# Key features of the late head pairs in strided order: key sums through one DRAM write and read, key-value sums placed by one transfer

## Chip, cores and metric

One core of a Trainium2 chip runs the kernel. The metric is the device time of one execution in microseconds (us); of several executions the median is taken. Before the change it is 1027.04 us, the median of 3 runs (1024.86 to 1032.23).

## What is computed

Linear attention with exponential features over 8 batches x 8 heads of 576 tokens with 64 values each, and then a two-layer feed-forward part over the 4608 tokens. All of it in float32:

```python
def phi(x):
    proj = np.einsum('bhsd,df->bhsf', x, w_phi)                 # 64 -> 128 features
    proj = proj - np.max(np.abs(proj), axis=-1, keepdims=True)
    return np.concatenate([np.exp(proj), np.exp(-proj)], axis=-1)
q_p, k_p = phi(q), phi(k)
kv  = np.einsum('bhsf,bhsd->bhfd', k_p, v)                      # key-value sums
z   = np.sum(k_p, axis=2)                                       # key sums
num = np.einsum('bhsf,bhfd->bhsd', q_p, kv)
den = np.einsum('bhsf,bhf->bhs', q_p, z)[..., None] + 1e-06
x   = (num / den), tokens x 512
out = relu(x @ w_in)**2 @ w_out                                 # 512 -> 2048 -> 512
```

The order in which the 128 features are summed doesn't matter to kv, num, z and den, as long as keys and queries meet feature by feature.

## The kernel before

**Work and stages.** Heads are handled in 32 pairs (`p`), four to a batch. The feed-forward part takes tokens in 18 chunks of 256 and its 2048 inner columns in 8 pieces (`f`); each (chunk, piece) is a first product on TensorE (L1028, 24 matmuls), squares on ScalarE (ACT, L1037 to L1047) with a difference on VectorE (DVE, L321), and a second product (L1066, 12 matmuls). For the last six chunks the first product is a Strassen form over two chunks at once (L1206). The weights arrive in 32-bit words of 8-byte elements and are joined and split in the first 120 us (L468 to L543).

**Early and late pairs.** Pairs 0 to 5 are "early": everything including the key sums is done with matmuls. Pairs 6 to 31 are "late". TensorE serves late pairs in "visits" (`visit`), each of which does three things for three neighbouring pairs: keys of pair p+1 (`k_main` L599 and `k_tail` L605, through `lhsT` = keys and `rhs` = the projection weights `wst` / `wbf`), queries and key-value sums of pair p (L869, L877, L657, L662), and numerators of pair p-1 (L889). A visit's keys then go through DVE (maximum L615, subtraction L618) and ACT (two exponentials, L621 and L623).

**Key sums of a late pair** (`late`). After DVE has folded the exponentials over tokens into `es` (L638 to L648), it transposes them in 32x32 blocks (L954) and sums rows (L955) into `z4`, 128 partitions x 16. What is left is a sum over four groups of 32 partitions, and a layout with one feature per partition. Four transfers (L961, `gather`) bring the four partition groups beside each other in `za` (32 partitions), DVE adds them (L968, `zr`), and four more transfers (L965, `column`) spread the result to `zc`, 128 partitions x 4. `zc` then scales the query features: ACT L990 and DVE L992, for each head; GpSimd (POOL) sums them over partitions (L996), and the denominators go through DRAM and back (L998, L805, L806, L809, L816) to DVE (L823), which divides; L842 and L845 write the result as two float16 halves into `ring`, from which the first product reads.

**Key-value sums of a late pair** (`turn`). DVE transposes them in 32x32 blocks (L938), one transfer writes them to DRAM (`td`, L939), and four transfers (L944, `place`) read them into `kz`, the stationary operand of the numerators, each for one block of 32 features.

**What sets the order.** Every instruction is an `Op` of a `Plan`: its engine, an expected duration, what it waits for, and for transfers an issue time and a landing time. `order` simulates the engines with these numbers and always takes the ready operation of lowest rank; ranks of the attention part come from the string `RANKS` (two characters each). The outcome is a fixed program order on each engine. Engines then run their own lists strictly in order: a transfer that waits in the SP queue holds all that are listed behind it, and so does a waiting instruction on ACT or DVE. All DMAs are issued from SP. Where the plan leaves TensorE idle in the first 125 us, `zeros` (L1314) fills in matmuls on zeros.

Of the kernel before, what the change touches and what calls it, by code (L numbers as in the profile page):

```python
# [307 lines left out]
def tile_kernel(ctx, tc, qp, kp, vp, w_phi, w_in, w_out, out):  # L308
    nc = tc.nc
    V, A, G, PE, SP = nc.vector, nc.scalar, nc.gpsimd, nc.tensor, nc.sync  # L310
    P = Plan()
# [16 lines left out]
    def tiles(pool, tag, shape, dtype, bufs, first=0):  # L328
        return Tiles(P, pool, tag, shape, dtype, bufs, first)
# [5 lines left out]
    wbf, wst = wraw[:, 0:2 * F], wraw[:, 2 * F:]  # L335
# [13 lines left out]
    es_ = tiles(ap, "es", [128, 1024], F32, 1, EARLY)  # L349
# [3 lines left out]
    kz_ = tiles(ap, "kz", [128, 384], F32, 2)  # L353
# [233 lines left out]
    exps, exp_t, sums, kz_of, qexp, dens_of, k_load, q_load, num_in = {}, {}, {}, {}, {}, {}, {}, {}, {}  # L587
# [5 lines left out]

    def k_main(p, to):
        for t in range(4):
            for h in range(2):
                PE.matmul(out=to(h)[:, 128 * t:128 * t + 128],  # L599
                          lhsT=k_[p][64 * h:64 * h + 64, 128 * t:128 * t + 128],  # L600
                          rhs=wst[64 * h:64 * h + 64, :], start=True, stop=True)

    def k_tail(p, to):
        for h in range(2):
            PE.matmul(out=to[64 * h:64 * h + 64, :], lhsT=k_[p][:, 512:576],  # L605
                      rhs=wbf[:, 128 * h:128 * h + 128], start=True, stop=True)
# [329 lines left out]
    def turn(p, v, key, src, rank):  # L936

        o = P.add("DVE", dve_us(256), lambda: V.transpose(kvs_[p][:, 0:256], src()), [v], [key, ("kvs", p)], rank)  # L938
        o = P.add("SP", 0.4, lambda: SP.dma_start(  # L939
            td_[p].rearrange("s p x -> p s x"), kvs_[p][:, 0:256].rearrange("p (s x) -> p s x", s=2)), [o], [("kvs", p), ("td", p)], rank, land=1.9, xfer=0.1)  # L940

        def place():
            for b in range(4):
                SP.dma_start(kz_[p][32 * b:32 * b + 32, 0:256].rearrange("p (a x) -> p a x", x=32),  # L944
                             td_[p].rearrange("s (a i) (b x) -> b i (s a) x", a=4, b=4)[b])

        kz_of[p] = P.add("SP", 1.9, place, [o], [("td", p), ("kz", p)], rank, land=1.5, xfer=0.4)

    def late(p):

        rank = PER_PAIR * p + RA
        R = lambda x: rank + x

        o = P.add("DVE", dve_us(512), lambda: V.transpose(es_[p][:, 512:1024], es_[p][:, 0:512]), sums[p], [("es", p)], R(RZ))  # L954
        o = P.add("DVE", dve_us(512), lambda: V.tensor_reduce(  # L955
            out=z4_[p], in_=es_[p][:, 512:1024].rearrange("p (b x) -> p b x", x=32), op=ALU.add, axis=AX.X),
            [o], [("es", p), ("z4", p)], R(RZ))

        def gather():
            for a in range(4):  # L960
                SP.dma_start(za_[p][:, a, :], z4_[p][32 * a:32 * a + 32, :])  # L961

        def column():
            for b in range(4):
                SP.dma_start(zc_[p][32 * b:32 * b + 32, :], zr_[p][:, 4 * b:4 * b + 4])  # L965

        o = P.add("SP", 1.6, gather, [o], [("z4", p), ("za", p)], R(RZ), land=1.9, xfer=0.1)
        o = P.add("DVE", 0.23, lambda: V.tensor_reduce(  # L968
            out=zr_[p].rearrange("p (b j) -> p j b", b=4), in_=za_[p].rearrange("p a (j b) -> p j b a", b=4), op=ALU.add, axis=AX.X),
            [o], [("za", p), ("zr", p)], R(RZ))  # L970
        zc = P.add("SP", 1.6, column, [o], [("zr", p), ("zc", p)], R(RZ), land=1.9, xfer=0.1)
        pt = pt_of[p]
        qexp[p], dens = [], []
        for h in range(2):
            n = 2 * p + h
            qe = lambda s, n=n: qe_[n][:, S * s:S * s + S]
            o = P.add("POOL", par_us(S), lambda n=n, h=h: G.partition_all_reduce(  # L977
                mx_[n], pt_[p][:, h, :], channels=128, reduce_op=bass_isa.ReduceOp.absmax),
                [pt[h], pt[2], pool_next], [("pt", p), ("mx", n)], R(RQ + 0.2), lock=1.0)
            o = P.add("DVE", dve_us(S), lambda n=n, h=h, qe=qe: sub(V, qe(0), pt_[p][:, h, :], mx_[n]),  # L980
                      [o], [("pt", p), ("mx", n), ("qe", n)], R(RQ + 0.3), lock=4.0)
            o = P.add("ACT", act_us(S), lambda qe=qe: A.activation(out=qe(1), in_=qe(0), func=AF.Exp, scale=-1.0),
                      [o], [("qe", n)], R(RQ + 0.4))
            o = P.add("ACT", act_us(S), lambda qe=qe: A.activation(out=qe(0), in_=qe(0), func=AF.Exp),
                      [o], [("qe", n)], R(RQ + 0.4))
# [3 lines left out]
            y = lambda h=h: (rb_, ds_)[h][p]  # L989
            o = P.add("ACT", act_us(S, 1), lambda h=h, qe=qe, y=y: A.activation(  # L990
                out=y(), in_=qe(0), func=AF.Copy, scale=zc_[p][:, 2 * h:2 * h + 1]), [zc, o], use, R(RQ + 0.8))
# [345 lines left out]

DIGITS = "".join(chr(c) for c in range(33, 127) if chr(c) not in "\"\\'")[:90]
RANKS = (
    ">i<,KT011@Odd$J72uZ6DE=3QkK9NWh|HZLvUfYqOs67=jqd@-<Z6JGO7ra68E7{aYQaV,cwW:l/IKE7C_jsE4@C/&m&g<F4LXb_"  # L1340
    "aQmB@tC.=*sX]hv:a6z:O^odzfit64YdXe/`Sl`#?]d]a4AW2eWS.cOUnGKdm{FzSS@Xp}/={$i+]Aa]?uI0q*K-B^v}P3IA82=v"
    "]@<OotUk{:PXG[4C.0R/N[/`fLEqW/F]vzg]=[H44Za`FqSl.-dDDu5d9N1mG5>_m37CDLmNN;sbrPEr@G/,?RZI2(BTddfmzups"
    "off5Jt?rLN?_qg:i8#67C0/=;vVd[SKVOv^Ow0.}7hLnN=N?X*@N`}5mNlIj=HCaBf<aMEdf.H2C8wCc.8R(5Sr]?Z.o_k7.5|xG"
    "BF8P47Z<Ov1(F4`A[9TdJ4fXcC642ql*hBA(BytbUUZ5e?Q>CqOOWniO3=E<NVJm=F:m0o7Th5pHwI<=u,I#^k=jK=B1R].-]@T|"
    "D:lh/v{kK4cX6Z49Sj2-NiKL.-j]0/U{fUG6.nv7Xz1/`7[*^c<(l8.Ps_pXK@.-A`0?P#.bC]C>^i3,AQ?`MzUIa!.-lrA*i-Ss"
    "B#?`GdE>L!0SX]SAQ:L.9GJ&;;hkI5RO;<O2L>|t{nL,9>I57`OFC(Gw`;|[.o89.kKixhhUw=H8s;G37WveEWf+]nLl;-QdI5XE"
    ":7@@JYH-1mxyU!V{UT.3kUKIFCa}q%<tD/ME0]3W0bEX@.|t0dmZmLILKmKR|t<Jp7<>F@9xscF)9,rJ34^fYeDLBnFt.IW>f7J&"
    "2hP}jYl.o`j<kKhsW%L5dc7MtF.->*VcEdCFDD_>1D<*os_^QVI)KZA3HTK(9tBrA.th;M=)VWqeV&Z6r*ZJ<XgkB9^mx[c+:M:1"
    "2^T/_|5E7$8fF^l4RTt>Ex3dH;D_RBig9HlOL;m|DfInD}CHC(DfW]UD7x1|=*yrvE<4Lmx[ZQLi/V.-0v.-N-jO1:.IsLMQp15u"
    "2bq{C#^iLN2YGYt6AMH}bQ@j;wkf1&BlU|d]7#TLPz<y?AiKY`V<L7RW]ye=V*].@9A[Iw@v?B_m/iM$tsA%YHbbI59]JO<)V]Y5"  # L1350
    "LwCWplB-fza>nyi<Lw<o3zZ4Ki8MV}@[HPW|>*dRpE.-|Q=5w:T@xNRDxnQs<6lftH<[fQ5{YDGU=Wo%1e{,Ku5+v@.-<<1RD<:>"
    "TvpT/t|t9(XFX@uYsaaW|tP)AZsqP.4@Ck[_BSa79VjkF>d}LiO%KL8H[&h]R0lZ?8Nbl(EN.zu-1d[[ExquOa97X(56EkG&7Md#"
    "?>.Y:PBmH6[1zeen:5b[H*cZ5u@yp?_r6>@)FW=o0VFa?^V:`1sRurr2gR``4P:$w;[Lpm?>3T.-JJ6.YW[G_Kzym%btEf.-=cIp"
    ";D:b:[v!6lJ?8Zk_3{Ef^DeWV4Mb.-f8=)i)hgJmXmwQO/H)f;|kRiV?GKFyDQC)O+i@zHr}QQ3hA&p?;ZCD8!Hn3y42hAc&D:{|"
    ".DF[<4s965sCKW=lqY]`2Z7@U6Vb@-^z<(GhbruKU@3b:_Wwq3j43=Po1tIwNyhzRW[,Axh#wRecP|9hgv]z88L)yTJWsT3#bF]9"
    "@3Ky.}/]QHT=0Zt7H/Sw18lF6@Ezohk8baLw<^TGf(7R]_rQFvQM2;EHeicW^?>ep*PD4rG6yD87P6.ZArbB6(0`U^ccBo>W5__H"
    "mtR.HcEkm$h}bw@5[[FWvA/5VF3sM>jeQ5^7E/J4R}ElFsGfZ/hKdO3LpZ2[Bcqfa2DoraU/zLV`K^m@OL5WEN7b<}8gvl5VT3Cn"
    "w>j?GXTo.IAx5qQiOf7t3d/ej+NBO9Ek4[{=3K_?X1rjakF(3a2TKDiN6I.-_WdTR8P,SqPbz:Bl.M1Yp&U]4:6s8K|kY^?A`%[z"
    "=`7lV#SuiX`F_K?Co8AAPIlw;f?-x2>$[(7).GStEHQ#NHeL.m2hN?UY_{XrXV1%5b:,L,|P3VQ&0Yoq>!mh7<Sf7!p:8:j0mb3F"
    "r$xp1n0)S0KMg[3#80E|hDggJd>EIRPonJF0CEhgI;:/f0EFa}tnn5uJi;j(wlA.:6/.YUJ6jEqPIr2HE2N1NhJQXDD-LtQu.1C0"  # L1360
    ".fmbTN|tY#UMFdn;YA.O3(0$ik4z|iMQ.01lgKe-eRNUMLxvv_qI?C[XZm;SD6WuMpr:I;<+7(Ex4i0ZZ0RlD;p;ZFt+cLKkY|=S"
    "/9n[TvQSj0|tcW"
)


# [31 lines left out]
```

## Time and profile before

| | |
|---|---|
| median of 3 runs | 1027.04 us (1024.86 to 1032.23) |
| the profiled execution | 1030.4 us, its span 1028.4 us |
| TensorE busy | 1005.6 us |
| DVE, ACT, POOL busy | 756.3, 674.3, 354.8 us |
| mean granted TensorE clock | 0.998 |
| DMA | 73.89 MB in 82629 packets, 51688 of them under 512 B |
| transfers per late pair that the change touches | 4 `za`, 4 `zc`, 4 `kz` |

In a row of groups stand the line, engine, operation, written and read tiles (buffer numbers left out; `z4` appears as `z`), shapes and count; then the busy time and the mean ns of one; then the idle time of that engine just before them, with what ended most of it. PEld is TensorE's weight load, SPq is a DMA issue in SP's queue. The chain of waits is followed back from the last instruction, at each step to what released it.

### The profile page before, as it was taken

The numbers are of one execution on the slowest core, as the hardware profiler recorded it, in microseconds if no ns is written. First come the engines' busy times: TensorE is split into PE (matmuls) and PEld (weight loads), VectorE is DVE, ScalarE is ACT, GpSimd is POOL, SyncE is SP. The second block draws the span as 40 slices with busy tenths as digits, with TensorE's granted clock in tenths as the row PEclk, the third lists the DMA queues.
The fourth block names the chain that finished last, engine by engine and source line by source line (L and its number), as shares of the span: only waits on it lengthen the run. The fifth ranks groups of instructions, "written<-read, shape, count | busy, mean of one in ns | idle before, by whom it ended". The sixth has DMA issues, their size and how long they took to land.

```text
span 1028.4 us, 19679 instructions
## 1 busy us (share of the span) xinstructions
PE 1005.6 (98%) x7664; PEld 688.8 (67%) x7744; DVE 756.3 (74%) x1196; ACT 674.3 (66%) x1194; POOL 354.8 (34%) x136
## 2 busy tenths in 40 slices
PE   7989999999999999999999999999999999999998
PEld 4657676666666666666666666666667667676775
DVE  6899898866984379798888988988966945443333
ACT  7889786756874477776876777765755545435444
POOL 2423356533652145664555655564220000000000
PEclk9999999999999999999999999999999999999999
DMA  9743413221411122241322332121010000000001
GB/s 357 277 166 120 165 56 85 71 74 29 126 54 50 40 74 73 60 121 33 111 71 70 84 100 70 48 56 28 13 39 21 1 1 36 7 1 21 21 1 41
DMA packets 82629, 73.89 MB, mean 72 GB/s; under 512 B 51688, under 2 KB 60520, under 8 KB 80488
## 3 DMA queue, kind: packets, MB, share of 16 engines
q1 hardware_dynamic: 82536, 72.63, 22.6%
q8 instruction: 61, 1.00, 0.4%
q14 instruction: 32, 0.26, 0.1%
HBM read 59.18 MB, written 12.99 MB: 70 GB/s over the span
## 4 chain that ended last, share of the span: by engine, by line
PE 84%; DVE 6%; ACT 4%; DMA 3%; issue 2%; SPq 1%; ACTq 0%; DVEq 0%
PE po L1066 27%; PE ph L1028 21%; PE pp L1206 6%; PE pz L657 4%; PE ph L1206 3%; PE pn L1066 3%; PE pv L1066 3%; PE pn L889 2%; PE pn L869 2%; PE pp L599 2%; PE pv L889 2%; PE pz L1206 2%; PE pz L662 1%; DVE ring L845 1%; PE pz L877 1%
## 5 line engine op out<-in xcount | busy, mean ns | idle before, releaser
L1028 PE MATMUL ph<-ring,win 128*128 128x256 f16 x2304 | 269.0, 274 | 2.8 <-ACT r L1037 2.8
L1028 PEld LDWEIGHTS <-win 128*128 128x128 f16 x2304 | 224.9, 98 | 51.4 <-issue 9.2
L977 POOL PARTITION_ALL_REDUCE mx<-pt x52 | 118.4, 2277 | 132.9 <-ACT pt L325 83.8
L1066 PE MATMUL po<-wh,gh 128*128 128x512 f32 x480 | 142.9, 418 | 0.5 <-ACT o L1085 0.5
L996 POOL PARTITION_ALL_REDUCE rb<-rb x26 | 97.2, 3744 | 124.6 <-DVE rb L992 113.3
L321 DVE TENSOR_TENSOR gl<-r,gh 128x512 bf16<-128x512 f32 x96 | 95.9, 999 | 48.2 <-ACT r L1047 47.3
L1066 PE MATMUL po<-wl,gl 128*128 128x512 bf16 x480 | 123.3, 379 | 0.0
L996 POOL PARTITION_ALL_REDUCE ds<-ds x26 | 96.4, 3709 | 55.3 <-DVE ds L992 55.3
L1037 ACT ACTIVATE r<-ph,cw 128x512 f32<-128x512 f32 x96 | 65.6, 683 | 75.7 <-PE ph L1028 75.2
L1066 PE MATMUL po<-wl,gh 128*128 128x512 bf16 x406 | 108.8, 381 | 5.1
L1066 PEld LDWEIGHTS <-gl 128*128 128x128 bf16 x576 | 56.3, 98 | 68.0
L1066 PEld LDWEIGHTS po<-wh,gh 128*128 128x128 f32 x480 | 81.8, 189 | 19.2 <-issue 5.4
L1066 PEld LDWEIGHTS <-gh 128*128 128x128 bf16 x576 | 44.7, 99 | 73.8 <-issue 40.4
L1238 ACT ACTIVATE qe<-qe,cw 128x512 f32<-128x512 f32 x48 | 34.1, 715 | 86.9 <-DVE qe L1221 86.9
L1221 DVE TENSOR_TENSOR qe<-pp,qe 128x512 f32<-128x512 f32 (+1 forms) x72 | 43.4, 602 | 58.6 <-PE pp L1206 56.9
L321 DVE TENSOR_TENSOR gl<-qe,gh 128x512 bf16<-128x512 f32 x48 | 33.2, 691 | 57.4 <-ACT qe L1047 57.4
L1045 ACT ACTIVATE gh<-r 128x512 fp32r<-128x512 f32 x96 | 60.5, 630 | 3.1
L1047 ACT ACTIVATE r<-r 128x512 f32<-128x512 f32 x96 | 60.5, 630 | 3.0
L621 ACT ACTIVATE e<-e 128x512 f32<-128x512 f32 x64 | 40.1, 626 | 26.7 <-DVE e L618 26.2
L657 PE MATMUL pz<-e,v 128*64 128x256 f32 x416 | 49.3, 379 | 0.0
L823 DVE TENSOR_TENSOR rb<-n,rb 128x576 f32<-128x576 f32 x32 | 36.7, 1148 | 17.0 <-DMA rb<-rd 16.7
L845 DVE SCALAR_TENSOR_TENSOR ring<-rb,cb,ring 128x576 f16<-128x576 f32 (+8 forms) x52 | 48.1, 943 | 1.3 <-ACT ring L842 1.2
(289 smaller groups left out, 1866.4 us busy)
## 6 DMA issues: line engine op xcount, KB each, us to landing
v<-in_vp_dram SPq DMA_DIRECT2D x32, 320.0 KB, 3.7
k<-in_kp_dram SPq DMA_DIRECT2D x32, 288.0 KB, 3.4
q<-in_qp_dram SPq DMA_DIRECT2D x32, 288.0 KB, 3.1
rb<-rd SPq DMA_DIRECT2D x64, 144.0 KB, 3.0
out_dram<-o SPq DMA_DIRECT2D x34, 256.0 KB, 2.1
td<-kvs SPq DMA_DIRECT2D x26, 128.0 KB, 2.6
kz<-td SPq DMA_DIRECT2D x104, 32.0 KB, 1.9
za<-z SPq DMA_DIRECT2D x104, 2.0 KB, 1.7
```

Of the source, the lines that this page charges most:

```text
L321: eng.tensor_tensor(out=out_, in0=a, in1=b_, op=ALU.subtract)
L657: PE.matmul(out=to[64 * h:64 * h + 64, 0:256], lhsT=v_[p][:, t, h, :], rhs=e_[2 * p + h][:, t].rearrange("p s f -> p (s f)"), start=t == 0 ...
L845: V.scalar_tensor_tensor(out=to(1), in0=rb_[p][:, c0:c1], scalar=cb[:, b, 1:2], in1=to(0), op0=ALU.mult, op1=ALU.subtract)
L977: o = P.add("POOL", par_us(S), lambda n=n, h=h: G.partition_all_reduce(mx_[n], pt_[p][:, h, :], channels=128, reduce_op=bass_isa.ReduceOp. ...
L996: o = P.add("POOL", 3.6, lambda y=y: G.partition_all_reduce(y(), y(), channels=128, reduce_op=bass_isa.ReduceOp.add), [o], [home], R(RQ + ...
L1028: PE.matmul(out=ph[:, j, :], lhsT=win[w][:, t, 128 * ff:128 * ff + 128], rhs=at_ring(c, x, t), start=k == 0, stop=k == 3 * KT - 1)
L1037: o = P.add("ACT", act_us(512, 1), lambda: A.activation(out=r_[n], in_=ph_[bank], func=AF.Relu, scale=cw[:, f, 0:1]), [g1], [("ph", bank), ...
L1045: sq = P.add("ACT", act_us(512), lambda: A.activation(out=gh_[n], in_=r(), func=AF.Square), after, use + [("gh", n)], Q)
L1047: o = P.add("ACT", act_us(512), lambda: A.activation(out=r(), in_=r(), func=AF.Square), [sq], use, Q, other=[("DVE", 0.70, lambda: V.tenso ...
L1066: PE.matmul(out=bank(i), lhsT=x[:, j, 128 * i:128 * i + 128], rhs=w[:, j, :], start=(ff == 0 and s == 0), stop=(ff == 2 * NFP - 1 and s == 2))
L1206: PE.matmul(out=to, lhsT=fl(x, *al)(k), rhs=fr(y, *ar)(k), start=n == 0, stop=n == 5)
L1221: V.tensor_tensor(out=to, in0=a, in1=b, op=ALU.add)
```

## The change

`mixed` reads the projection weights for the keys of late pairs with a step of four: moving column 32b+i of `wst` and `wbf` is feature 4i+b. Late keys' features thus come out in another order, and the four partition groups of `z4` and the blocks of `td` now hold features that are neighbours in the wanted layout. So one access pattern whose partition step is constant covers all 128 partitions, where four transfers were needed:

- `zd`, a new DRAM scratch tile: `z4` is written to it by one transfer of 128 rows x 16 values, and read back by one transfer of 128 x 4 x 4 values (pieces of 16 bytes) into `za`, now 128 partitions x 4 x 4. DVE adds over the four groups straight into `zc`. `zr`, `gather` and `column` are gone.
- `kz` is read by one transfer of 128 partitions x 8 x 32 values (1024 pieces of 128 bytes) instead of four of 32 partitions.
- DVE's row sums (L955) write `z4` with a step.
- The expected issue and landing times of the plan are changed with it, and `RANKS` is a new list, so the order of the attention part changes on all engines.

```diff
-    za_ = tiles(sm, "za", [32, 4, 16], F32, 1, EARLY)
-    zr_ = tiles(sm, "zr", [32, 16], F32, 1, EARLY)
+    za_ = tiles(sm, "za", [128, 4, 4], F32, 1, EARLY)
...
+    zd_ = tiles(dr, "zd", [128, 16], F32, 2, EARLY)
...
+    def mixed(p, w):
+        return w if p < EARLY else w.rearrange("p (i b) -> p b i", b=4)
+
     def k_main(p, to):
...
-                          rhs=wst[64 * h:64 * h + 64, :], start=True, stop=True)
+                          rhs=mixed(p, wst[64 * h:64 * h + 64, :]), start=True, stop=True)
...
-                      rhs=wbf[:, 128 * h:128 * h + 128], start=True, stop=True)
+                      rhs=mixed(p, wbf[:, 128 * h:128 * h + 128]), start=True, stop=True)
...
-        def place():
-            for b in range(4):
-                SP.dma_start(kz_[p][32 * b:32 * b + 32, 0:256].rearrange("p (a x) -> p a x", x=32),
-                             td_[p].rearrange("s (a i) (b x) -> b i (s a) x", a=4, b=4)[b])
-
-        kz_of[p] = P.add("SP", 1.9, place, [o], [("td", p), ("kz", p)], rank, land=1.5, xfer=0.4)
+        kz_of[p] = P.add("SP", 0.55, lambda: SP.dma_start(
+            kz_[p][:, 0:256].rearrange("p (a x) -> p a x", x=32), td_[p].rearrange("s (a i) (b x) -> (i b) (s a) x", a=4, b=4)),
+            [o], [("td", p), ("kz", p)], rank, land=2.2, xfer=0.5)
...
-            out=z4_[p], in_=es_[p][:, 512:1024].rearrange("p (b x) -> p b x", x=32), op=ALU.add, axis=AX.X),
+            out=z4_[p].rearrange("p (b c) -> p c b", c=4), in_=es_[p][:, 512:1024].rearrange("p (c b x) -> p c b x", c=4, x=32), op=ALU.add, axis=AX.X),
...
-        o = P.add("SP", 1.6, gather, [o], [("z4", p), ("za", p)], R(RZ), land=1.9, xfer=0.1)
-        o = P.add("DVE", 0.23, lambda: V.tensor_reduce(
-            out=zr_[p].rearrange("p (b j) -> p j b", b=4), in_=za_[p].rearrange("p a (j b) -> p j b a", b=4), op=ALU.add, axis=AX.X),
-            [o], [("za", p), ("zr", p)], R(RZ))
-        zc = P.add("SP", 1.6, column, [o], [("zr", p), ("zc", p)], R(RZ), land=1.9, xfer=0.1)
+        o = P.add("SP", 0.4, lambda: SP.dma_start(zd_[p], z4_[p]), [o], [("z4", p), ("zd", p)], R(RZ), land=1.9, xfer=0.1)
+        o = P.add("SP", 0.55, lambda: SP.dma_start(za_[p], zd_[p].rearrange("(a i) (b c) -> (i b) a c", a=4, b=4)),
+                  [o], [("zd", p), ("za", p)], R(RZ), land=2.2, xfer=0.3)
+        zc = P.add("DVE", 0.23, lambda: V.tensor_reduce(
+            out=zc_[p], in_=za_[p].rearrange("p a c -> p c a"), op=ALU.add, axis=AX.X),
+            [o], [("za", p), ("zc", p)], R(RZ))
```

Line numbers of the changed program differ: up to L595 they agree but for the tile declarations near L362, from L602 to L945 they are 3 higher than before, L954 and L955 keep theirs, and from L975 on they are 7 lower.

**Where the order moves: SP around pair 9.** The names carry the pair: `q_11`, `k_12`, `v_14` are loads, `td_3` and `kz_9` are the key-value sums of pair 9, `za_3`, `zr_3`, `zc_3`, `zd_3` and `ds_3` belong to pair 9 too, `rd_8`, `rb_8` and `den_8` to the denominators of pair 8. Before:

```order
L961 DMA za_3_2499<-z4_3_2492 32x16 x4
L592 DMA q_11_2520<-in_qp_dram 128x576
L591 DMA k_12_2526<-in_kp_dram 128x576
L554 DMA v_14_2534<-in_vp_dram 128x640
L809 DMA rd_8_2566<-rc_8_2531 128x9
L939 DMA td_3_2571<-kvs_9_2564 128x2x128
L944 DMA kz_9_2596<-td_3_2571 32x8x32 x4
L816 DMA rb_8_2380<-rd_8_2566 64x576 x2
L965 DMA zc_3_2644<-zr_3_2608 32x4 x4
```

Now:

```order
L959 DMA zd_3_2435<-z4_3_2419 128x16
L960 DMA za_3_2459<-zd_3_2435 128x4x4
L591 DMA k_12_2505<-in_kp_dram 128x576
L592 DMA q_11_2507<-in_qp_dram 128x576
L554 DMA v_14_2509<-in_vp_dram 128x640
L991 DMA den_8_2544<-rb_8_2441 64x1x9
L942 DMA td_3_2553<-kvs_9_2548 128x2x128
L991 DMA den_8_2544<-ds_2_2438 64x1x9
L945 DMA kz_9_2578<-td_3_2553 128x8x32
```

The second half of pair 9's key sums stood last, behind the loads, `td`, four `kz` and two `rb`; now the last transfer of the key sums stands ahead of the loads, and nothing of them follows on SP.

**ACT at the same place.** `qe` are the query features of pair 9, `r` and `gh` the squares of the feed-forward part; the rows that read `zc_3` are the ones that need the key sums. Before:

```order
L982 ACTIVATE qe_19_2610<-qe_19_2610 128x576
L1037 ACTIVATE r_17_2670<-ph_22_2615,cw_82 128x512
L1045 ACTIVATE gh_17_2673<-r_17_2670 128x512
L1047 ACTIVATE r_17_2670<-r_17_2670 128x512
L990 ACTIVATE rb_9_2701<-qe_18_2573,zc_3_2644 128x576
L984 ACTIVATE qe_19_2610<-qe_19_2610 128x576
L990 ACTIVATE ds_3_2707<-qe_19_2610,zc_3_2644 128x576
L621 ACTIVATE e_21_2577<-e_21_2577 128x4x128
L1037 ACTIVATE r_18_2725<-ph_23_2676,cw_82 128x512
```

Now:

```order
L1030 ACTIVATE r_17_2640<-ph_22_2583,cw_82 128x512
L1038 ACTIVATE gh_17_2642<-r_17_2640 128x512
L1040 ACTIVATE r_17_2640<-r_17_2640 128x512
L975 ACTIVATE qe_19_2621<-qe_19_2621 128x576
L977 ACTIVATE qe_19_2621<-qe_19_2621 128x576
L983 ACTIVATE ds_3_2676<-qe_19_2621,zc_3_2489 128x576
L977 ACTIVATE qe_18_2575<-qe_18_2575 128x576
L983 ACTIVATE rb_9_2692<-qe_18_2575,zc_3_2489 128x576
L1030 ACTIVATE r_18_2695<-ph_23_2650,cw_82 128x512
```

The users of `zc_3` stay between the same two feed-forward pieces (17 and 18); the keys' exponentials of pair 10 (`e_21`) have moved ahead of this place.

**DVE in the first 83 us.** `wl0` and `wh0` are weight halves (casts of 128x1024), `ring0` is the first ring write. Before:

```order
L565 TENSOR_REDUCE m1_1_99<-vm_1_371 128x1
L529 CAST wl0_634<-u_2_539 128x1024
L475 SCALAR_TENSOR_TENSOR u_3_657<-u_3_657,raw2i_169 128x1024
L475 SCALAR_TENSOR_TENSOR u_4_670<-u_4_670,raw1o_199 128x1024
L823 TENSOR_TENSOR rb_0_640<-n_0_496,rb_0_640 128x576
```

Now:

```order
L732 TENSOR_REDUCE qm_3_673<-ph_3_641 128x4
L475 SCALAR_TENSOR_TENSOR u_3_658<-u_3_658,raw2i_161 128x1024
L475 SCALAR_TENSOR_TENSOR u_4_676<-u_4_676,raw1o_195 128x1024
L826 TENSOR_TENSOR rb_0_651<-n_0_498,rb_0_651 128x576
```

A cast has gone from this place. Ahead of the fourth pair's ring write (L845 before, L848 now) DVE has 124 instructions before and 123 now: two `wl` casts fewer and one `wh` cast more, the rest alike.

**What the order leaves alone.** TensorE has the same matmuls in both programs, apart from six more on zeros in the first 83 us. On SP the 12 transfers of each late pair become 3. Before the last ring writes of the first batch, ACT has the same 108 instructions.

More of the change, by code (lines that the diff above doesn't have):

```diff
@@ L955, in late @@
         o = P.add("DVE", dve_us(512), lambda: V.tensor_reduce(
-            out=z4_[p], in_=es_[p][:, 512:1024].rearrange("p (b x) -> p b x", x=32), op=ALU.add, axis=AX.X),
+            out=z4_[p].rearrange("p (b c) -> p c b", c=4), in_=es_[p][:, 512:1024].rearrange("p (c b x) -> p c b x", c=4, x=32), op=ALU.add, axis=AX.X),
             [o], [("es", p), ("z4", p)], R(RZ))
[L959 to L965, printed above, removed]
-        o = P.add("SP", 1.6, gather, [o], [("z4", p), ("za", p)], R(RZ), land=1.9, xfer=0.1)
-        o = P.add("DVE", 0.23, lambda: V.tensor_reduce(
-            out=zr_[p].rearrange("p (b j) -> p j b", b=4), in_=za_[p].rearrange("p a (j b) -> p j b a", b=4), op=ALU.add, axis=AX.X),
-            [o], [("za", p), ("zr", p)], R(RZ))
-        zc = P.add("SP", 1.6, column, [o], [("zr", p), ("zc", p)], R(RZ), land=1.9, xfer=0.1)
+        o = P.add("SP", 0.4, lambda: SP.dma_start(zd_[p], z4_[p]), [o], [("z4", p), ("zd", p)], R(RZ), land=1.9, xfer=0.1)
[4 more added lines that the diff above has]
+            [o], [("za", p), ("zc", p)], R(RZ))
         pt = pt_of[p]
@@ L1339 @@
 RANKS = (
[L1340 to L1359, printed above, removed]
@@ L1360 @@
-    "r$xp1n0)S0KMg[3#80E|hDggJd>EIRPonJF0CEhgI;:/f0EFa}tnn5uJi;j(wlA.:6/.YUJ6jEqPIr2HE2N1NhJQXDD-LtQu.1C0"
-    ".fmbTN|tY#UMFdn;YA.O3(0$ik4z|iMQ.01lgKe-eRNUMLxvv_qI?C[XZm;SD6WuMpr:I;<+7(Ex4i0ZZ0RlD;p;ZFt+cLKkY|=S"
-    "/9n[TvQSj0|tcW"
+    ":4;uIk3?S_rN@MV..-uU:|FwW+E=JjOO?7^LKD{KIn5#RBnXvMgilo2)2pv34`A8BVwTIU]pRljEObC}5Any6aHD<NI%q$sesn3I"
+    "9axuOL9@dsZ37!p-NS4)P7_T{!Hq9(5Qfm2VNW0|iWz#|s6f8ZrCcOVQizaoi|Ats5G|H=yqdK_qE47Pi,Oiivc#JiD.kurV^m88"
+    "vmV&L-G(RB3h>e?%A9:VPT.1WCP7o,7.T)am7QsY<7i]d+YH0eX@;hJ9R+ttBkf2r#5u9vg{Fno,Dn1O[eL*KYk</&V99H^O=BI2"
@@ new lines @@
+    "Cie.5<M;R=a_w47[4l_BVcQ86yL+>iOAl;7Wvu=B`D?#KXP.?RTm`]ad_IHB5i;L@hS8cEj6Dk:&NWc4hn.E1mHdn,kc2m_92RGI"
+    "EdUs3qwxF>HPNFCt>AK,.mXs^fqxa+F6a:M33IFA>Y.-I]k767P+_WK0K6Rg2]oHI#C:=NF`NzhdU2k`IyC`4gAzBgw^Sy=BmJfG"
+    "{93IT3N&4xtK`bSpi+1z<-YFELHGce:s6*Xvqs]8..4DJgpF2RbL;TRF<9K//@rWB0h>RvWO?V8a7GS[_hp5M&4|DSBYnw;N3cND"
+    "YMcHMET|=K@6[{A&VB3+GT=]7(hzrH;&9>1d3bYxZWCHQUFEkShHek?JR)Jt^oP-V;l_w/AF6^8J<d4>5nyr=^q$QRY0<@K2LI{?"
+    "PmNzT7P/_D|i]MJ)E(EF^Ed}?5S|]AJb;tL)H^3PqaL#G%pPc?QengME33VY|2zqZn_nU1NL7)1;qE8[hvt&JB]79_{/7jd?_%6_"
@@ new lines @@
+    "[$vtQ}|Jb]Q0u=FXS;.-@niYko^s3z1g_?Q{;W4XPHc(6/DN82MFUTicQVRC9}/@.j;YBAQ[^RMdRT3geU;QJR@DvdNQPL4sd?OJ"
+    "YQ;!CSkl/^l>QfcGFSHSFOv.d-7V<@0$^.jl8:j#VeY*aM:jLi>6qhgKYCl,U*Q7l!fyF[7S]3t_e64?DMknP}HOt>H[C>W^_&o<"
+    "?^LdT[AEKX5R1x?#_l7.DZ;&O.xMazH{Y{D!pHUwD^1/2TpW:%0]Eh`[?|?.jK6AIbMYt&y/DjS.LPKUNEU<XzWXKMOdnJtxLVR`"
+    "R6prc`xmC*qfHVW`Nj;5WF<OE$BqI`_8l^<G:f^MB_:fBx88GoIuDJdirKrLr0j%hRBnal/,p?1A3WsSSiFXO_]/9IMip2>+7!5^"
+    "Mr:aPM<C:jxaP[d,vzE2_#{oO|]u<93H]qwvAD4UZ<wDLY7WJl2Odo4+/L/4QMw2dlt!goMVmvKYM8rp4-q,3<S6KD>E^8]s:j;<"
@@ new lines @@
+    "[0VEVn[D6z_W0B<|hJ7=z-?^CBMFYmOhEVj!1Iyd:@69zXMY@0]SMsZ*2ogT?oqEH@_=y{|skzV:L&IgrUMdP}N2GdDt1)OTW7b5"
+    "I|Ho@oI)Ar?pN4|t5W8`3HhiJ{LV4.gO0&19Q%5jwZJ3ad;RMMC%P}XEJxGq[GT+.q_;Z|mBsO[qeTc/O5^g.qwSEqPSCk^U?<kV"
+    "t?|tXUBtOUWzA|Qwz]C%n+2opHe/3_`Q1WLp:kzI6i3B?gSj`S2NvV2:o09huMyhfZ/o@7[5:p2+N<2}0?yPf[U:u<2pl:1RiLc,"
+    "42se]NNVwZQoM^S9ExA[>y|2:@Zmv8OmN3qRt>e,GaC=@WJN;jK1=A?OY!A]uMgBVQJc:+/Y4LQYwk.-<-=[U?|m5WnCHI|tjMnn"
+    "D+I85%_;Ms.RVwrZ4n9@7k^_>B>U<x?6W(IQ/V5P</<;Z8^01q1(XYD@>%@WQ{0_rb9|I&2H]Gdz{K7cH;ZerT7gFm[VTQ8wmdVG"
@@ L1363 @@
+    "P!>Sq$.-3{AEB5RB[]5wx.m_0ez+KR_2^N;IGOP#_IA`uBQC|6;+9_>=Wa0JGMSHR}F8Kg96NAT_nd.k;0?ks60c3[::cdXQ1:IY"
+    "RCDd=rKsY-L`d[S_U:Jl{hS.fKp:5uQtP1.Bl`Gy>aQ?:LswX:0Hjj|t6IWAFxbyt?J3tOiHHjW0OKJ5F-T2.eme:T>fU)2-RIXt"
+    "JAzBOh9*V8`=U$UD>Ome2|bu5%35MqR1n55p=<wPgxZ$E/YbGxYhpZq$^RFf4)B@M6AqGHc[>*pV^jJ5]o<f<;3)bPBJ`A4xdtw0"
+    "yw=bm<eD?446ZVFxpaTK.I2njD7h|t3H9ypAj^3P?IzHNS|tV(zI[KLY5YvzeUY;BWzWsB9XVjpaeJ|te+rY;P2[GPp5S!l;A[PL"
+    "WcHF2eu5J!WNe4"
 )
```

## Prediction

> **What bounds the kernel now.** I read the page first: shares of the span and the chain that ended last.
>
> ```profile
> PE 1005.6 (98%) x7664; PEld 688.8 (67%) x7744; DVE 756.3 (74%) x1196; ACT 674.3 (66%) x1194; POOL 354.8 (34%) x136
> PE 84%; DVE 6%; ACT 4%; DMA 3%; issue 2%; SPq 1%; ACTq 0%; DVEq 0%
> ```
>
> TensorE is busy for all but 22.8 of 1028.4 us, and 84% of the chain is TensorE following itself. The late pairs' transfers aren't a bound by themselves: a shorter chain of transfers gains only where TensorE stands still because of it. So the second view is the windows, cut where TensorE first runs dense and around its largest gap. Behind the stretch and its length stand the busy times of PE, PEld, DVE, ACT and POOL, then the granted clock and the DMA share.
>
> ```profile
> 0.00:83.10 83.10, 73.10 (x848) 46.12 (x851) 68.65 (x126) 67.98 (x128) 23.28 (x22) 1.00 0.68 251
> 83.10:214.00 130.90, 130.29 (x1003) 90.34 (x1011) 108.19 (x170) 100.87 (x176) 60.62 (x24) 1.00 0.32 100
> 214.00:219.00 5.00, 2.94 (x15) 1.53 (x15) 2.58 (x4) 3.25 (x6) 1.65 (x1) 1.00 0.27 102
> 219.00:223.40 4.40, 4.40 (x26) 3.06 (x25) 4.40 (x3) 1.75 (x3) 4.40 (x2) 0.61 0.01 1
> 223.40:1028.40 805.00, 794.91 (x5781) 547.77 (x5846) 572.48 (x897) 500.50 (x884) 264.80 (x89) 1.00 0.17 49
> ```
>
> Ten idle microseconds lie in the first 83, before any late pair has keys; the change touches them only through the new list. The window at 219 shows something else: TensorE is busy throughout and yet slow, at a granted clock of 0.61. The waits after 83 us (in total, times, longest) say who is to blame:
>
> ```profile
> PE ph L1028 <- ACT r L1037: 2.8, 2, 2.0
> PE po L1066 <- ACT o L1085: 0.5, 1, 0.5
> PE pn L869 <- DVE pw L416: 0.2, 1, 0.2
> ```
>
> That is 3.5 us; the windows leave some 9 us more idle after 83 us, for which no engine is named: pieces between blocks and the last store. Two of the three are ACT handing over late. ACT is only 66% busy, so I follow the largest back along the chain of waits:
>
> ```profile
> 210.35 0.59 SPq L965
> ...
> 212.26 3.27 DMA zc<-zr
> ...
> 215.63 0.79 ACT rb L990
> ...
> 218.37 0.58 ACT r L1037
> ...
> 218.99 4.45 PE ph L1028 x24
> ```
>
> and in the timeline, with the gaps:
>
> ```profile
> 205.79 0.24 DVE L968 TENSOR_REDUCE zr<-za 32x16 f32<-32x64 f32 x1
> 207.28 1.80 SPq L944 DMA_DIRECT2D kz<-td  x4
> 211.54 2.78 PE L1028 MATMUL ph<-ring,win 128*128 128x256 f16 x24
> 215.63 0.78 ACT L990 ACTIVATE rb<-qe,zc 128x576 f32<-128x576 f32 x1 [4.55 <-DMA zc<-zr]
> 218.99 4.45 PE L1028 MATMUL ph<-ring,win 128*128 128x256 f16 x24 [2.00 <-ACT r L1037]
> ```
>
> Pair 9's partial sums `zr` are done at 206.0, but their four spreading transfers are issued only from 210.35 on, behind four `kz` and two `rb`; `zc` lands at 215.5. ACT stands for 4.55 us at L990, with the next feed-forward piece's `r` listed behind it, and TensorE for 2.00 us behind that. Then the same 24 matmuls take 4.45 us instead of 2.78: the granted clock is down. The place costs 2.0 + 1.7 = 3.7 us, the largest single loss after the start.
>
> The Trainium skill (TensorE: Matmul & The Clock Gate, The HAM clock gate) puts the drop to half rate behind about 3.4 us of idle; here 2.0 us were enough, so the row decides. By that rule removing the wait would give 2.0 us and not 3.7.
>
> **The change part by part.**
>
> *Key sums, transfers.* The first late pair (6) shows the whole old chain with little else in the queue:
>
> ```profile
> 115.78 0.69 DVE L955 TENSOR_REDUCE z<-es 128x16 f32<-128x512 f32 x1
> 116.49 2.49 SPq L961 DMA_DIRECT2D za<-z  x4
> 120.47 0.26 DVE L968 TENSOR_REDUCE zr<-za 32x16 f32<-32x64 f32 x1 [0.51 <-DMA za<-z]
> 120.75 2.42 SPq L965 DMA_DIRECT2D zc<-zr  x4
> ```
>
> and the page gives the landings, counted from the issue:
>
> ```profile
> td<-kvs SPq DMA_DIRECT2D x26, 128.0 KB, 2.6
> kz<-td SPq DMA_DIRECT2D x104, 32.0 KB, 1.9
> za<-z SPq DMA_DIRECT2D x104, 2.0 KB, 1.7
> zc<-zr SPq DMA_DIRECT2D x104, 0.5 KB, 1.7
> rd<-rc SPq DMA_DIRECT2D x32, 4.5 KB, 1.9
> ```
>
> Old: from 116.47 to 120.75 + 2.42 - 0.6 + 1.7 = 124.3, which is 7.8 us (the last of four issues begins some 0.6 before their end). New: the write `zd` is like `rd` (128 small rows to DRAM), 1.9; the read `za` has no row of its kind, 512 pieces of 16 bytes, and lies between `za`'s 1.7 and `td`'s 2.6; the sum on DVE 0.25. Together 3.9 to 4.8 us, so 3 to 4 us shorter. SP is held for the wait between the two transfers, some 2 us, where it spent 4.9 us on eight issues. Listed behind the waiting `za` are loads for pairs 11, 12 and 14, which visits after the next one use, and pair 8's denominators and pair 9's `td`, which wait for other engines at that place anyway. Without that cover 2 us of TensorE and its slow clock would be at stake, 3.7 us, as in the rival below.
>
> *Key-value sums.* One `kz` issue instead of four: at least 1.3 us less of the SP queue (1.80 us for four above). One transfer of 1024 pieces may land later than one of 256: 1.9 to, say, the 3.7 us that the four took together from first issue to last landing (1.80 + 1.9). It doesn't matter: pair 9's `kz` landed near 211, and its numerators come at the end of a visit whose keys TensorE reads from 224.5 on (a row further down). Cost nothing, cover 13 us; if that were gone, 2 us.
>
> *The large wait.* In the new list pair 9's `zc` is a DVE instruction far ahead of its user on ACT, and `za` stands ahead of the loads on SP. To keep this wait the chain would have to be later than before although it lost both its four issues and the queue ahead of them. I take out all 3.7 us. What is late next is the DVE step L985 behind it; it has to share with GpSimd's sums either way.
>
> *The smaller waits.* The second on ACT `o` (0.5 us) has four `zc` issues in its chain too:
>
> ```profile
> 316.37 1.35 SPq L965
> ...
> 319.72 0.54 SPq L816
> ...
> 320.30 2.91 DMA rb<-rd
> ...
> 324.82 0.59 ACT o L1085
> ```
>
> Without 2.4 us of issues ahead of `rb` it would go. The remaining 0.8 us on `r` hangs on a long chain. Against these stands that a new list has small waits of its own; bounds are +2 and -1.5, and I take -0.7.
>
> *The start.* Ahead of the fourth pair's ring write, which lets the first product begin, DVE has one cast less net:
>
> ```profile
> L529 DVE CAST wl<-u 128x1024 bf16<-128x1024 f32 x3 | 2.7, 888 | 0.0
> ```
>
> 0.9 us, in a stage where DVE is busy for 68.65 of 83.1 us. Bounds: the reshuffled ranks can move this by 3 us either way (a third of the 10 us that TensorE idles there). I take -0.9. The six more matmuls on zeros fill idle time.
>
> *The strided read.* `mixed` lets TensorE read 128 moving columns with a step of 16 bytes, 8 matmuls of `k_main` and 2 of `k_tail` in each of 26 visits. From the same chain, further on:
>
> ```profile
> 224.50 0.89 PE pp L599 x16
> ...
> 225.77 0.22 PE pz L605 x4
> ```
>
> These take 0.89 + 0.22 = 1.11 us per visit, 28.9 us in all, and TensorE has no slack to hide more. Nothing in this trace reads moving data with such a step. The nearest rows are on DVE:
>
> ```profile
> L955 DVE TENSOR_REDUCE z<-es 128x16 f32<-128x512 f32 x26 | 17.7, 682 | 0.6
> L968 DVE TENSOR_REDUCE zr<-za 32x16 f32<-32x64 f32 x26 | 6.4, 246 | 15.6 <-DMA za<-z 15.6
> L565 DVE TENSOR_REDUCE m<-vm 128x1 f32<-128x4 f32 x8 | 1.2, 149 | 0.0
> ```
>
> Over the short L565, 508 more contiguous elements cost 533 ns, 1.05 each; L968's 60 more, read with a step of 64 bytes, cost 97 ns, 1.6 each. TensorE reads one column of these float32 matmuls in 0.11 us / 128 = 0.87 ns (16 records in 0.89 us, two at a time on different rows). If a stepped read could deliver no more than one per 1.6 ns there too, the 28.9 us would become 53, +24 us. At the other end it costs nothing: the second product takes 12 matmuls of 512 columns, four of them with 4-byte operands, in 2.67 us,
>
> ```profile
> 94.79 2.67 PE po L1066 x12
> ```
>
> which is 0.43 ns a column. So the keys' 0.87 ns is the pace of the several passes of a float32 product and not that of the read, and the read has room. L968's groups of four are a poor likeness for rows of 32. I take 0 and keep +24.
>
> The Trainium skill (Advanced Engine Details and Errata, SBUF Cachelines) says that lines are 16 bytes and that at least two reads should fall into one, or the memory's latency shows. A step of exactly four float32 values gives one, so this page speaks against the change; by it the sum would be that of the first rival below. L968 agrees with it on DVE; no row here shows it on TensorE.
>
> *Sum.* -3.7 - 0.7 - 0.9 + 0 = -5.3 us: span 1028.4 to 1023.1. The profiled execution took 1030.4 us, 3.4 above the median of 1027.0, and the waits differ between executions; I take the difference over to the median: 1021.7, rounded **1022 us**.
>
> **Rivals.**
>
> *The strided read is slow (slower).* Mechanism and price as above: every visit grows by 0.9 us on a busy TensorE, 1022 + 24 = 1046. For it: L968's rate, and that TensorE can't hide it. Against: the columns' slow pace. From 0.2 us per visit on (5.3 us) it outweighs the gain, from 0.6 on (15 us) the loss can be told.
>
> *The waits move.* DVE now stands at `zc` for two transfers in a row if the list puts it too early. Already L968 cost DVE 15.6 us of waiting over 26 pairs (its row above). DVE hands `gl` to TensorE; one gap of 2 us with its slow clock costs 3.7. Then the gain is used up: 1022 + 3.7 or + 7.4, 1026 to 1029. Against: at pair 9 eight DVE instructions stand between the row sums and `zc`, about as long as the new chain.
>
> *More is gained.* All 3.5 + 1.7 us after the start and a good half of the 10 us before it: 1027 - 5.2 - 5 = 1017 or less. For it only that the list is new everywhere; the start's idle time hangs on weight and key loads, which don't change.
>
> *The shorter chain isn't there.* If the 16-byte pieces land as late as eight transfers did, `zc` still isn't behind `rb` in the queue; then about 1024, within the forecast's spread.
>
> **How the numbers follow.** Forecast 0.61 (with the last rival in it), waits move 0.12, strided read 0.20, more gained 0.07. A measurement of this kernel tells about 1% (10 us) from no change. Faster by more: 0.08, the third rival and a tail. Slower by more: 0.19, nearly all of the strided read. Within 1%: 0.73. The range begins at 1016, where the most that waits and start can give ends, and reaches to 1040, which takes in moved waits and a mild cost of the strided read (up to two thirds of its price); left out are 0.16 above and 0.03 below.
>
> **What would show it.** Right: the 24 key matmuls of a visit (L602, L608) still 0.89 and 0.22 us apart in the chain; no window with a clock of 0.6 after the start; ACT without a wait for `zc` over 1 us; three transfers per late pair, `za` landing within 2.6 us; TensorE busy about 1004 us. Wrong: L602 near 1.6 us per visit, or a new wait of 2 us on `r` or `gl` with a slow block behind it, or a first product that begins later than 85 us.

## The result and the profile after

The changed kernel takes 1054.15 us (median of 4 runs, 1053.27 to 1055.68) against 1026.84 us before (4 runs, one more than above): a ratio of 1.0263, 95% interval 1.0242 to 1.0283. The likeliest case of the forecast was 1022 us; the first rival, the slow stepped read, was priced at 1046.

The profiled execution has a span of 1051.8 us, 23.4 more than that of before. Its page, with the same rows as those shown of before:

```profile
PE 1035.2 (98%) x7668; PEld 705.9 (67%) x7750; DVE 737.9 (70%) x1192; ACT 676.2 (64%) x1197; POOL 360.8 (34%) x137
PE 94%; DMA 4%; ACT 1%; issue 1%; DVE 0%; SPq 0%; ACTq 0%
```

TensorE is busy for 29.6 us more with nearly the same matmuls, and now makes up 94% of the chain instead of 84%: less waiting, longer work. The windows, cut at the same places up to 214 us, say the same:

```profile
0.00:83.10 83.10, 75.59 (x855) 47.08 (x861) 67.16 (x125) 68.61 (x128) 24.36 (x23) 1.00 0.70 252
83.10:214.00 130.90, 130.38 (x964) 89.39 (x971) 101.78 (x169) 97.47 (x171) 62.76 (x24) 1.00 0.32 100
214.00:600.00 386.00, 384.07 (x2819) 261.25 (x2846) 300.00 (x478) 267.67 (x493) 193.69 (x64) 1.00 0.27 73
600.00:1051.80 451.80, 445.16 (x3038) 308.17 (x3075) 268.98 (x421) 242.45 (x408) 79.95 (x26) 1.00 0.09 26
```

The granted clock stays at 1.00, and the view of TensorE's waits after 83 us, which named 3.5 us before, is empty. So what the shorter transfers were to do has happened. Where the time went shows in the groups of the late keys' matmuls, before:

```profile
L599 PE MATMUL pp<-wraw,k 64*128 64x128 f32 x432 | 28.8, 273 | 0.0
L605 PE MATMUL pz<-wraw,k 128*64 128x128 f32 x104 | 10.2, 275 | 0.0
```

and after:

```profile
L602 PE MATMUL pp<-wraw,k 64*128 64x128 f32 x432 | 52.7, 396 | 0.0
L608 PE MATMUL pz<-wraw,k 128*64 128x128 f32 x104 | 16.2, 397 | 0.0
```

The same counts take 23.9 + 6.0 = 29.9 us more. In the chain one visit's keys stand at 1.81 and 0.45 us, where 0.89 and 0.22 stood. The prediction had named "L602 near 1.6 us per visit" as a sign of being wrong:

```profile
157.32 1.81 PE pp L602 x16
...
159.51 0.45 PE pz L608 x4
```

The transfers themselves, issue to landing:

```profile
kz<-td SPq DMA_DIRECT2D x26, 128.0 KB, 2.5
...
zd<-z SPq DMA_DIRECT2D x26, 8.0 KB, 1.4
za<-zd SPq DMA_DIRECT2D x26, 8.0 KB, 1.8
```

With the sum on DVE

```profile
L962 DVE TENSOR_REDUCE zc<-za 128x4 f32<-128x16 f32 x26 | 4.3, 167 | 0.4 <-DMA za<-zd 0.4
```

the new key sums take 1.4 + 1.8 + 0.2 = 3.4 us where the old took 7.8, and DVE's waiting for them fell from 15.6 us to 0.4. The 3.4 us hold when DVE is free: in pair 6, the pair of the 7.8, `za` has landed at about 134.7 us, but DVE is at other work and comes to the sum at 136.7, so that `zc` is written 5.4 us after the row sums.

### The profile page after: what moved, and what is told of

Same layout as the page of the kernel before. It is cut to its first block, busy times and chain, and to the rows that moved or that the text cites. A ratio compares the mean times of both kernels' runs of the same rounds, so it can differ in the third digit from the quotient of the medians.

```text
span 1051.8 us, 19258 instructions
## 1 busy us (share of the span) xinstructions
PE 1035.2 (98%) x7668; PEld 705.9 (67%) x7750; DVE 737.9 (70%) x1192; ACT 676.2 (64%) x1197; POOL 360.8 (34%) x137
## 4 chain that ended last, share of the span: by engine, by line
PE 94%; DMA 4%; ACT 1%; issue 1%; DVE 0%; SPq 0%; ACTq 0%
PE po L1059 30%; PE ph L1021 24%; PE pp L1199 6%; PE pp L602 5%; PE pz L660 4%; PE ph L1199 3%; PE pn L1059 3%; PE pv L1059 3%; PE pn L892 3%; PE pn L872 3%; PE pv L892 2%; PE pz L1199 1%; DMA k<-in_kp_dram 1%; DMA raw2i<-in_w_in_dram 1%; PE pz L608 1%; PE pz L665 1%
## 5 line engine op out<-in xcount | busy, mean ns | idle before, releaser
L618 DVE TENSOR_REDUCE km<-pp 128x4 f32<-128x512 f32 x54 | 36.5, 681 | 46.2 <-PE pp L602 45.9
L602 PEld LDWEIGHTS pp<-wraw,k 64*128 64x128 f32 x432 | 43.9, 199 | 14.8 <-issue 11.5
L602 PE MATMUL pp<-wraw,k 64*128 64x128 f32 x432 | 52.7, 396 | 0.0
```

The costliest lines, as they stand in the source:

```text
L602: PE.matmul(out=to(h)[:, 128 * t:128 * t + 128], lhsT=k_[p][64 * h:64 * h + 64, 128 * t:128 * t + 128], rhs=mixed(p, wst[64 * h:64 * h + 6 ...
```

## Experiments

Theory A: all of the loss is the stepped moving read of the late keys' weights. Rival B: the new order or the new transfers cost the time, and the slower keys only fill room that is there.

**The change without the stepped read.** The weights are copied once into the new order:

```diff
+    wmix = cp.tile([128, 3 * F], F32, name="wmix")
...
+        G.tensor_copy(out=wmix.rearrange("p (g b i) -> p g b i", g=3, b=4), in_=wraw.rearrange("p (g i b) -> p g b i", g=3, b=4))
...
-                          rhs=mixed(p, wst[64 * h:64 * h + 64, :]), start=True, stop=True)
+                          rhs=late_w(p)[64 * h:64 * h + 64, 2 * F:], start=True, stop=True)
```

(`k_tail` likewise; `late_w(p)` is `wraw` for early pairs and `wmix` for late ones.)

> The changed kernel, but the projection weights of the late keys are copied once, in the new feature order, to a contiguous tile (one GpSimd copy of 128x384 at the start); every engine's list is otherwise that of the change. Theory A (all of the loss is the stepped moving read): a visit's keys fall back from 1.91 + 0.44 to 0.99 + 0.22 us, 26 x 1.135 = 29.5 us are gained, 1054.2 - 29.5 = 1024.7 us (up to 1027, if waits come back that the longer visits had covered), that is 0 to 0.3% under the kernel before. Rival B (the loss comes from the new order or the new transfers, the slower keys only fill the room): stays above 1045 us. Of the forecast only the small gain would remain in A; by its sum this kernel is at 1022.

Measured: 1023.93 us (median of 9, 1022.82 to 1026.08) against 1027.01 before on the same chip (14 runs), ratio 0.9965, interval 0.9951 to 0.9979. The copy costs 0.87 us on GpSimd at a time when it waits for the first weights anyway:

```profile
9.81 0.87 POOL L398 COPY wmix<-wraw 128x384 f32<-128x384 f32 x1
11.56 1.17 POOL L477 TENSOR_SCALAR raw0i<-raw0i 128x1024 int32<-128x1024 uint32 x1 [0.88 <-DMA raw0i<-in_w_in_dram]
```

and the keys are back at the old pace:

```profile
222.28 0.89 PE pp L606 x16
...
223.56 0.22 PE pz L612 x4
```

A holds, B falls. (The expectations count a visit's main keys until the next matmuls begin, 1.91 and 0.99 us; the chain's rows give 1.81 and 0.89. The difference is the same.) This version also beats both kernels, by 0.35% (interval above) against before, which is small but clear of the noise, and by 30 us of medians against the change.

**The stepped read alone, in the kernel before.**

```diff
+    def stepped(p, w):
+        return w if p < EARLY else w.rearrange("p (i b) -> p b i", b=4)
...
-                          rhs=wst[64 * h:64 * h + 64, :], start=True, stop=True)
+                          rhs=stepped(p, wst[64 * h:64 * h + 64, :]), start=True, stop=True)
```

> The kernel before, with the stepped read of the weights for late keys and nothing else (key and query features then meet in different orders, so what is left of the result is the time). Theory A: the keys of a visit take 1.91 + 0.44 us, + 29.5 us, 1056 us, or a few us less where the longer visits cover waits of before (1052 to 1057). Rival B: within 5 us of the kernel before.

Measured: 1056.62 us (median of 4, 1053.98 to 1058.69), ratio 1.0283, interval 1.0254 to 1.0313, which is 29.6 us over before, as theory A expected. Nothing else of the change is in this kernel, and its two groups of late keys are those of the changed kernel to the last digit, 52.7 and 16.2 us. The two results add up: + 29.6 for the read and - 3.1 for the rest make + 26.5, and the change measured + 27.3.

**Other steps.** What is it in the step? `b=4` in `mixed` becomes 2 (8 bytes), then 8 (32 bytes; only the first edit is shown):

```diff
-        return w if p < EARLY else w.rearrange("p (i b) -> p b i", b=4)
+        return w if p < EARLY else w.rearrange("p (i b) -> p b i", b=2)
```

> The change with a step of 2 values (8 bytes) in place of 4 (16 bytes) in the moving read; the features land in another order, so only the time counts. If what costs is that each read opens a new 16-byte line (theory L): two reads fall into a line, 0.99 + 0.22 us per visit, about 1025 us. If any step other than 1 costs (rival S): 1.9 + 0.44 us as with 4, about 1054 us.

> The change with a step of 8 values (32 bytes) in the moving read; the features land in another order, so only the time counts. Theory L (one new line per read, whatever the distance): 1.91 + 0.44 us per visit as with 4, about 1054 us. Rival G (the cost grows with the distance): over 2.5 us for the main part, over 1070 us.

Measured, one run each: 1024.23 us with 8 bytes, 1055.01 us with 32. The groups, for 8 bytes:

```profile
L602 PE MATMUL pp<-wraw,k 64*128 64x128 f32 x432 | 29.2, 272 | 0.0
L608 PE MATMUL pz<-wraw,k 128*64 128x128 f32 x104 | 10.4, 278 | 0.0
```

and for 32 bytes:

```profile
L602 PE MATMUL pp<-wraw,k 64*128 64x128 f32 x432 | 53.9, 402 | 0.0
L608 PE MATMUL pz<-wraw,k 128*64 128x128 f32 x104 | 16.4, 402 | 0.0
```

So a step as such costs next to nothing (29.2 against 28.8), and a step of 32 bytes costs hardly more than one of 16 (53.9 against 52.7): theory L, one new 16-byte line per read, against S and G.

**Is it a rate of lines, or a factor of two?** For that another pace of data is needed: the first product with 2-byte values, in the kernel before (the second run has `b=8`).

```diff
-                                  rhs=at_ring(c, x, t), start=k == 0, stop=k == 3 * KT - 1)
+                                  rhs=at_ring(c, x, t).rearrange("p (i b) -> p b i", b=4), start=k == 0, stop=k == 3 * KT - 1)
```

> The kernel before; the first product of chunks 0 to 11 (L1028, 2304 float16 matmuls of 256 moving columns) reads `ring` with a step of 4 values, 8 bytes (the tokens of a chunk come out in another order, no work is left out). This asks what of the stepped read is the rule for 2-byte data, whose contiguous pace is 0.106 us per matmul, 0.41 ns a column. Theory L (a new 16-byte line can be had every 1.7 ns, as the float32 step of 16 bytes showed: 0.92 + 0.99 us for 8 x 128 columns on two row groups): two reads per line, 0.83 ns a column, 0.21 us per matmul, + 245 us, about 1270 us. Rival H (two reads per line are enough at any pace): 1027 us.

> As the one before, with a step of 8 values, 16 bytes, one read per line. Theory L: 1.7 ns a column, 0.43 us per matmul, + 740 us, about 1770 us. Rival H (a read that opens a new line takes twice the time of one that doesn't, whatever the data's pace): 0.21 us per matmul, about 1270 us.

Measured, one run each: 1295.46 us with 8 bytes and 1982.69 us with 16. One piece's 24 matmuls in the chain, with 8 bytes:

```profile
214.13 5.54 PE ph L1028 x24
```

with 16 bytes:

```profile
200.90 10.85 PE ph L1028 x24
```

and before, contiguous:

```profile
83.22 2.73 PE ph L1028 x24
```

10.85 us / (24 x 256) is 1.77 ns for a column that opens a line each time. With two columns per line, 5.54 us give 0.90 ns a column, 1.80 ns a line. The float32 keys: 1.81 us / (8 x 128) = 1.77 ns, and the tail 0.45 / (2 x 128) = 1.76 ns. (Each of these matmuls leaves two records in the trace, and the records begin in pairs some 6 ns apart, so 16 records take 8 turns of 128 columns.) One number fits all within 2%: about 1.77 ns per new 16-byte line of the moving operand, for both types. Rival H falls: two reads per line, free for the float32 keys, double a 2-byte product. The total with 8 bytes is above the expected 1270 because that was worked out with 1.7 ns (the expectation's own 0.92 + 0.99 us over 8 x 128 columns would have given 1.87). With 16 bytes the first product explains some 790 of the 954 us (2304 matmuls that begin 452 ns apart instead of 109); the rest is paid elsewhere, since the granted clock fell to 0.752 on the mean.

**Which part of the rest gains?** The contiguous version with the ranks of the kernel before, and the kernel before with the new ranks; in each only the text of `RANKS` is exchanged. The order is made anew from ranks and expected durations.

> The contiguous copy with the new transfers, but with the list of ranks of the kernel before. Theory T (the small gain of the contiguous version, 3 us, comes from the shorter transfers that take the late waits away): 1024 us, like the contiguous version. Rival O (it comes from the new list): 1027 us, like before, or above, as the list was made for other durations.

> The kernel before (old transfers, contiguous weights) with the new list of ranks alone. Theory T: no gain, 1027 us or above, since the list now counts on transfers that are shorter than these are. Rival O: 1024 us.

Measured, beside 1028.48 us for the kernel before (17 runs): 1026.08 us with new transfers and old ranks (12 runs, ratio 0.9982, interval 0.9968 to 0.9995), and 1072.08 us with old transfers and new ranks (5 runs, ratio 1.0418, interval 1.0388 to 1.0447). So the transfers gain about 2 us even with ranks made for longer ones, and the new ranks gain nothing by themselves: without the short transfers they lose 43.6 us. Whether the ranks add to the transfers' gain (0.9965 against 0.9982, intervals that overlap) stays open. Where the time goes with old transfers and new ranks, TensorE's waits after 83 us:

```profile
PE pn L889 <- ACT pt L325: 18.1, 4, 10.4
PE pn L410 <- DVE m L565: 10.8, 1, 10.8
PE ph L1028 <- ACT r L1037: 2.0, 1, 2.0
...
```

Nearly all of these lie between 409 and 477 us; from 409 to 478 TensorE is idle for 33.8 of 69 us, and its granted clock is 0.77. SP's queue there, in the timeline:

```profile
414.70 2.46 SPq L961 DMA_DIRECT2D za<-z  x4
418.22 0.33 SPq L809 DMA_DIRECT2D rd<-rc  x1
418.70 3.09 SPq L965 DMA_DIRECT2D zc<-zr  x4
421.88 0.53 SPq L939 DMA_DIRECT2D td<-kvs  x1
422.51 1.11 SPq L816 DMA_DIRECT2D rb<-rd  x2
423.88 1.85 SPq L944 DMA_DIRECT2D kz<-td  x4
```

Sixteen issues stretch over 11 us, 9.4 of them spent issuing, and the denominators and loads listed behind them come after. That this starts the waits is argued from the rows; no run takes it apart, and there is a rival: the chain of waits from 395 to 480 us gives GpSimd's sums and maxima (L996, L977) 26% and the `za` issues 4%.

**The kernel before, profiled again.**

> The kernel before, unchanged, for a second profile. The contiguous version gained 3.1 us where the sum of the forecast without the stepped read was -5.3. Theory V (the 3.7 us wait with its slow clock, which the first profile shows at 214 to 223 us, is not in every execution, and the profiled one was a slow one): here TensorE waits less than 2 us in all after 83 us, and the span is 1025 us or less. Rival N (it is always there, and something else of the sum was missed): 2.0 us of idle time before L1028 and a window at half clock again, span about 1028 us.

Measured: span 1024.8 us (1026.85 us in all). TensorE's waits after 83 us:

```profile
PE ph L1028 <- ACT r L1037: 0.8, 1, 0.8
PE po L1066 <- ACT o L1085: 0.5, 1, 0.5
PE pn L869 <- DVE pw L416: 0.3, 1, 0.3
```

and at the place of the large wait:

```profile
208.52 1.13 SPq L816 DMA_DIRECT2D rb<-rd  x2
209.69 2.51 SPq L965 DMA_DIRECT2D zc<-zr  x4
213.42 0.78 ACT L990 ACTIVATE rb<-qe,zc 128x576 f32<-128x576 f32 x1 [2.52 <-DMA zc<-zr]
216.78 2.78 PE L1028 MATMUL ph<-ring,win 128*128 128x256 f16 x24
```

Theory V: ACT still waits for `zc`, but 2.52 us instead of 4.55, since `zc` came some 2 us earlier this time; what reaches TensorE is too small for a row, and the clock stays up. So the 3.7 us are not in every execution. They may not be rare: of the 31 executions of the kernel before that were timed beside the other runs, 10 list a mean granted clock of 0.998 or less, as the first profiled one did, and among these are all seven above 1030 us. No trace shows which wait it was in those.

## Why the prediction was wrong

*What bounds.* Right: TensorE follows itself, and the transfers matter only through its waits.

*The strided read.* This is the step that failed. The text took 0 and kept +24 us; it is +29.6 (the stepped read alone). What spoke for 0 was a row of the second product, 12 matmuls of 512 contiguous columns in 2.67 us, "0.43 ns a column", hence "the read has room". That compares columns. Counted in lines the same row says the opposite: four 4-byte columns share a 16-byte line, and the 4-byte matmuls of this product begin 231 ns apart in the same trace (median), 1.80 ns for each of their 128 lines, which is the very rate that the experiments found as the limit. The contiguous keys, at 0.87 ns a column, open a line every 3.5 ns and so have room for twice as many; a step of 16 bytes asks for four times as many, one line per 0.87 ns, and gets one per 1.77, so the keys take twice as long. The row that argued against the rival was already at the limit. The other row, L968 on DVE with 1.6 ns per read of a new line, came within a tenth of it, and was set aside as a poor likeness; whether the two engines share a cause, no run shows. The rule of the Trainium skill (Advanced Engine Details and Errata, SBUF Cachelines) that two reads should fall into a line agrees for float32 (8 bytes free, 16 bytes doubled); for the 2-byte product two reads per line were not enough, 5.54 against 2.73 us.

*The chances.* With the rival's mechanism right in place and near in size (1046 forecast, 1054 measured), its chance of 0.20 looks too low: a rule, and the only row with reads of new lines, spoke for it, and against it one misread row. The range ended at 1040 and left it out. (The "24 key matmuls of a visit" among the signs are a slip: it is 8 + 2, which leave 20 records.)

*Key sums and key-value sums.* Right, and the chain is shorter still: 3.4 us against 3.9 to 4.8 forecast, since the write `zd` lands after 1.4 us and not 1.9; `za` at 1.8, inside its bounds; `kz` at 2.5, and no engine waits for it.

*The large wait.* The mechanism was right, the size was not: it is gone from the changed kernel, but -3.7 us was the price in the profiled execution. In the second profile of before it is below a row. The forecast carried it over to the median although the profiled execution took 3.4 us more than the median, nearly the size of the wait itself.

*The smaller waits.* -0.7 was a little small: 1.6 us of named waits in the second profile of before, none in the contiguous version.

*The start.* Taken at -0.9. The cast is gone, and the first product begins at 82.8 us where it began at 83.15 and 82.98 in the two profiles of before. But in the other traces it begins anywhere between 82.3 and 83.9 us with the old ranks and, with the new ranks and transfers, between 82.1 and 83.0, so a gain of 0.9 us can't be told from this scatter.

*The sum without the read.* -5.3 us forecast, -3.1 measured (contiguous version). Less the 3.7 us, which the second profiled execution didn't pay, the forecast would have been -1.6.

*The waits move.* Did not happen: DVE waits for `za` 0.4 us in all.

## What to carry to other kernels

Before a moving operand is read with a step, count the 16-byte lines it opens, not its columns: on TensorE one new line took 1.77 ns, so a float32 product at 0.87 ns a column tolerated a step of 8 bytes and doubled at 16, and a 2-byte product at 0.43 ns a column doubled already at 8. By the same count a 4-byte operand read at 0.43 ns a column has no room for any step; no run here tries that. Where the same stepped operand is used again and again, copy it once into the order wanted; here 0.87 us on an idle engine saved some 30. And a wait that is read from one profile is worth its price only if a second execution shows it too: compare the profiled time with the median before it goes into the sum.

## What the runs showed of the hardware

- Contiguous data can be at the same limit. In the second product, matmuls of 512 contiguous columns begin 231 ns apart (median, kernel before) with 4-byte values, 128 lines at 1.80 ns, and 216 ns apart with 2-byte values, half as many lines. In the trace of the 16-byte step on the 2-byte product, where the granted clock was 0.5, both begin 427 ns apart: with that much time per column the lines no longer show.
- The limit isn't TensorE's clock. With the 16-byte step on the 2-byte product the clock was at half for about half of the run, while TensorE was busy all the time:

```profile
300.00:600.00 300.00, 300.00 (x1004) 112.94 (x1001) 97.85 (x168) 92.67 (x171) 68.11 (x24) 0.71 0.12 33
```

  In the trace of that run nine in ten of the 2304 matmuls still begin about 450 ns after the one before, at either clock. So the profile can show a TensorE as busy that is held up by its reads inside the matmuls, and that is granted less clock. That the reads brought the clock down is a reading of this one run: with the 8-byte step, at 227 ns a matmul, the clock stayed at 1.00. The second product, which reads contiguously, then paid too:

```profile
L1066 PE MATMUL po<-wh,gh 128*128 128x512 f32 x480 | 225.6, 610 | 0.0
```

  against, in the kernel before,

```profile
L1066 PE MATMUL po<-wh,gh 128*128 128x512 f32 x480 | 142.9, 418 | 0.5 <-ACT o L1085 0.5
```

- In the first profile of before, 2.0 us without a matmul were followed by some 3.4 us at half the granted clock (4.45 us for 24 matmuls instead of 2.78).
